# Two key loads split into bands of 112, 8 and 8 partitions in a two-layer decode kernel

## The chip, the cores and the metric

The kernel runs on one core of a Trainium2 chip. The metric is the device time of one execution in microseconds (us). The core has sixteen DMA engines that move data between the chip's main memory (HBM) and the on-chip memory of 128 partitions, and five instruction streams: TensorE (PE in the profile), VectorE (DVE), ScalarE (ACT), GpSimd (POOL) and SyncE (SP). In this kernel SP does nothing but issue DMA transfers.

## The reference

Two layers, each attention over a cached context followed by a gated MLP, are applied to two sequences of one new token each. The same weights serve both layers.

```python
def _A_ref(x, k_cache, v_cache, wq, wo):          # D = 576, H = 32, Sk = 8192, Dh = 128
    q = (x @ wq).reshape(B, Sq, H, Dh).transpose(0, 2, 1, 3)
    scores = einsum("bhqd,bhkd->bhqk", q, k_cache) * (Dh ** -0.5)
    p = softmax(scores)
    o = einsum("bhqk,bhkd->bhqd", p, v_cache)
    return o.transpose(0, 2, 1, 3).reshape(B, Sq, H * Dh) @ wo

def _B_ref(x, w_gate, w_up, w_down):              # Df = 4608
    return (gelu(x @ w_gate) * (x @ w_up)) @ w_down

x = x + _A_ref(layernorm(x), ...); x = x + _B_ref(layernorm(x), ...)
x = x + _A_ref(layernorm(x), ...); x = x + _B_ref(layernorm(x), ...)
```

The key cache and the value cache have 2 x 32 heads of 8192 x 128 float32 values, 256 MiB each, and both layers read all of them. With the weights that is over a gigabyte per execution, and each value is used once per layer, so the work per byte is small.

## The kernel before

The unit of attention work is an `Item`: one sequence and two neighbouring heads (30 items, `PAIRS`), or one head for the last four items. The keys of a pair are 8 MiB and land as a tile of 128 partitions, each of which holds 128 rows of 128 values, 64 KB in one piece. The values of a pair have the same form.

All large tiles live in one buffer, `space`, cut into slots by hand. The class `Arena` keeps account of which parts are free. The functions `plan_first`, `plan_second` and `plan_mlp` append loads to a list in the order in which they are to be issued; `pump` issues from its head for as long as the arena has room, and `done` frees a part and calls `pump` again. So the order of the loads on SP's queue is written out by hand, and each issue waits on SP until the work that last read its place in `space` has ended. In layer 0 the items go from 0 up, and the order is key n, then value n - 1. In layer 1 they go down: key n, then value n + 1. There is room for three pair tiles, so an 8-MiB load is issued while the one or two before it are still on their way.

For each item, VectorE multiplies the keys by the query (line 511), GpSimd adds the two halves of each row (line 515), and VectorE sums the rest (line 518). A short softmax follows on VectorE, TensorE and ScalarE, and TensorE multiplies the weights with the values (line 604). After the last item of a layer, the output weights (`out_rows`, line 281) are multiplied in at line 657, `add_to_x` adds to x, and the MLP streams gate, up and down weights (lines 228 to 263). In layer 0's MLP the gate and up weights are loaded by `split_rows` in transfers to every second partition (line 238).

The lines that the change touches are `load` (line 163, its DMA at line 166), which issues one transfer, `cache` (line 168), which makes the list entry for a whole item, and one call in each of `plan_first` and `plan_second`.

Of the kernel before, what the change touches and what calls it, by code (L numbers as in the profile page):

```python
# [15 lines left out]
P = 128  # L16
# [8 lines left out]
JC = 16  # L25
# [15 lines left out]
NPLACE = 4  # L41
RING = 5 * SLOT
END = RING + NPLACE * PLACE
HELD = 5


# [13 lines left out]
ITEMS = [Item(b, h, 2) for h in range(0, H - 2, 2) for b in range(B)]  # L60
# [7 lines left out]
class Arena:  # L68
# [38 lines left out]
    def fit(self, key, n, lo=0):  # L107

        for at in [self.at, lo] + sorted(end for _, end in self.live.values()):
            if lo <= at and at + n <= END and self.take(key, at, n) is not None:  # L110
                self.at = at + n
# [11 lines left out]
def decode_layers(ctx, tc, x_in, kc, vc, wq, wo, wg, wu, wd, out):  # L123
    nc = tc.nc
# [8 lines left out]

    space = consts.tile([P, END], F32, name="space")

    x = consts.tile([P, CW], F32, name="x")
    nc.vector.memset(x, 0.0)
    for c in range(4):
        for s in range(2):
            lo = 32 * c + s * B  # L140
# [16 lines left out]
    def part_at(at, n):  # L157
        return space[:, at:at + n]
# [1 line left out]
    def part(at):  # L160
        return part_at(at, PART).rearrange("p (j d) -> p j d", d=DH)

    def load(at, n, src, lo, hi):

        t = part_at(at, (hi - lo) * PART).rearrange("p (j d) -> p j d", d=DH)
        nc.sync.dma_start(t, ITEMS[n].source(src)[:, lo * JC:hi * JC, :])

    def cache(key, src, n, slots=None, pieces=None):

        parts = ITEMS[n].parts  # L170

        def make():
            at = arena.pair(key) if slots is None else arena.slots(key, slots, parts)
            if at is None:
                return False
            lo = 0
            for m in pieces or (parts,):
                load(at[lo], n, src, lo, lo + m)
                lo += m
            ready[key] = dict(enumerate(map(part, at)))  # L180
            places[key] = at
            return True

        queue.append(make)

    def half(key, src, n, k, slot):

        def make():
            at = arena.slots(key, (slot,), 4, k)
            if at is None:  # L190
                return False
            load(at[0], n, src, k, k + 4)
            ready.setdefault(key, {}).update((k + i, part(a)) for i, a in enumerate(at))
            return True

        queue.append(make)

    def one(key, src, n, k, where):

        def make():  # L200
            at = arena.ring((key, k), PART) if where is None else arena.take((key, k), places[where[0]][where[1]], PART)
            if at is None:
                return False
            load(at, n, src, k, k + 1)
            ready.setdefault(key, {})[k] = part(at)
            return True

        queue.append(make)
# [13 lines left out]
    def half_rows(key, w, us, first):  # L222

        width = w.shape[1] // 2
        rows = w.rearrange("r (s w) -> (r s) w", w=width).rearrange("(p u) w -> p u w", p=P)

        def transfers(t):
            nc.sync.dma_start(t.rearrange("p (u w) -> p u w", w=width), rows[:, us[0]:us[-1] + 1, :])

        weights(key, len(us) * width, first, transfers)  # L230
# [36 lines left out]
    def products():  # L267

        def make():
            at = [RING + k * PLACE for k in (2, 3)]  # L270
            if not all(arena.clear(a, PLACE) for a in at):
                return False
            ready["products"] = [part(arena.take(("products", k), at[k], PART)) for k in range(2)]
            return True

        queue.append(make)

    def out_rows(layer, g):

        rows = wo[g * GH * DH:(g + 1) * GH * DH, :].rearrange("(p i) c -> p (i c)", i=GH)  # L280
        weights(("wo", layer, g), GH * D, whole_at[layer], lambda t: nc.sync.dma_start(t, rows))
# [14 lines left out]
    def groups(layer):  # L296
        return range(H // GH)[::1 - 2 * layer]

    def name(kind, layer, n):

        return kind, 1 if n in (KEYS_HELD if kind == "k" else VALUES_HELD) else layer, n

    def plan_first():
        def k(n, *at):
            cache(name("k", 0, n), kc, n, *at)

        def v(n, *at):
            cache(name("v", 0, n), vc, n, *at)

        for us in WQ[0]:  # L310
            half_rows(("wq", 0, us[0]), wq, us, END - NU * H * DH // 2)
        last = PAIRS - 1
        k(0)
        for n in range(1, PAIRS):
            k(n)
            v(n - 1)
        k(SINGLE[0], (0,))
        half(("v", 0, last), vc, last, 0, 1)
        half(("v", 0, last), vc, last, 4, 5)
        k(SINGLE[1], (3,))  # L320
        v(SINGLE[0], (4,))

        k(SINGLE[2], (2,))
        products()
        k(SINGLE[3], (0,))
        v(SINGLE[1], (4,))
        v(SINGLE[2], (3,))
        for g in groups(0)[:2]:
            out_rows(0, g)
        v(SINGLE[3], (1,), (1,) * 4)  # L330
        for g in groups(0)[2:]:
            out_rows(0, g)

    def plan_second():
        for us in WQ[1]:
            half_rows(("wq", 1, us[0]), wq, us, None)
        last = PAIRS - 1
        k63, v63, k62, v62 = ("k", 1, SINGLE[3]), ("v", 1, SINGLE[3]), ("k", 1, SINGLE[2]), ("v", 1, SINGLE[2])
        for k in range(4):
            one(("k", 1, SINGLE[1]), kc, SINGLE[1], k, None)  # L340
        for k in range(4):
            one(("k", 1, SINGLE[0]), kc, SINGLE[0], k, (k63, k))

        for kind, k in (("k", 0), ("v", 0), ("v", 1), ("k", 1), ("v", 2), ("v", 3), ("k", 2), ("k", 3)):
            if kind == "k":
                one(("k", 1, last), kc, last, k, (k62, k))
            else:
                one(("v", 1, SINGLE[0]), vc, SINGLE[0], k, (v63, k))
        for k in range(4):
            one(("k", 1, last), kc, last, 4 + k, (v62, k))  # L350
        half(("k", 1, last - 1), kc, last - 1, 0, 5)
        half(("k", 1, last - 1), kc, last - 1, 4, 4)
        cache(("v", 1, last), vc, last)
        for n in range(last - 2, -1, -1):
            cache(("k", 1, n), kc, n)
            cache(("v", 1, n + 1), vc, n + 1)
        cache(("v", 1, 0), vc, 0, None, (4, 2, 1, 1))
        for g in groups(1):
            out_rows(1, g)

    def plan_mlp(layer):
# [11 lines left out]
        for rows in DOWN[layer]:  # L373
            down(layer, rows)

    plan_first()
    plan_mlp(0)
    plan_second()
    plan_mlp(1)
    pump()  # L380
# [453 lines left out]
```

## Time and profile before

| what | value |
|---|---|
| median of 3 runs | 2697.15 us (2696.98 to 2701.9) |
| the profiled execution | 2700.58 us, its span 2698.8 us |
| VectorE busy | 1872.1 us, 69% of the span |
| GpSimd busy | 1210.8 us, 45% |
| TensorE busy | 900.1 us, 33% |
| read from HBM | 1154.23 MB, 428 GB/s over the span |

The profile follows one execution. Its page gives each engine's busy time, the span in 40 slices with a digit for the busy share in tenths (9 is 90% or more), the DMA queues (q1 is the kernel's own hardware queue issued from SP; the two others that matter here, marked "instruction", fetch the engines' programs), and the chain of work that ended last, followed back from the end. In the chain and in the timelines a row begins with its start and its length in us. The DMA view can be asked for a window of the span; its digits and counts are then of that window, cut into 40 slices again. "Under 512 B" counts the smallest packets, nearly all of them the writes that report a transfer's completion.

### The profile page before, as it was taken

The numbers are of one execution on the slowest core, as the hardware profiler recorded it, in microseconds if no ns is written. First come the engines' busy times: TensorE is split into PE (matmuls) and PEld (weight loads), VectorE is DVE, ScalarE is ACT, GpSimd is POOL, SyncE is SP. The second block draws the span as 40 slices with busy tenths as digits, with TensorE's granted clock in tenths as the row PEclk, the third lists the DMA queues.
The fourth block names the chain that finished last, engine by engine and source line by source line (L and its number), as shares of the span: only waits on it lengthen the run. The fifth ranks groups of instructions, "written<-read, shape, count | busy, mean of one in ns | idle before, by whom it ended". The sixth has DMA issues, their size and how long they took to land.

```text
span 2698.8 us, 17988 instructions
## 1 busy us (share of the span) xinstructions
PE 900.1 (33%) x7020; PEld 294.0 (11%) x7020; DVE 1872.1 (69%) x1688; ACT 90.0 (3%) x399; POOL 1210.8 (45%) x528
## 2 busy tenths in 40 slices
PE   1323331333233223334644332333233323322355
PEld 0100010001000000111211110001000100000022
DVE  4877787678777776776039887778767867777740
ACT  0000000000000000000000000000000000000000
POOL 2644454445445444544016554445444544544420
PEclk7656656665666566666766665665566566656677
DMA  9999999999999999999999999999999999999998
GB/s 420 435 434 434 434 434 433 433 432 434 435 433 432 435 432 430 433 428 422 403 378 421 429 427 436 435 430 434 434 434 431 434 434 432 434 433 436 432 421 378
DMA packets 33524, 1155.39 MB, mean 428 GB/s; under 512 B 3976, under 2 KB 4000, under 8 KB 5536
## 3 DMA queue, kind: packets, MB, share of 16 engines
q1 hardware_dynamic: 33400, 1154.24, 99.5%
q8 instruction: 55, 0.90, 0.1%
q14 instruction: 29, 0.24, 0.0%
q10 hardware_dynamic: 40, 0.01, 0.0%
HBM read 1154.23 MB, written 0.00 MB: 428 GB/s over the span
## 4 chain that ended last, share of the span: by engine, by line
DMA 82%; DVE 15%; PE 1%; issue 1%; POOL 1%; ACT 0%; SPq 0%; ACTq 0%; DVEq 0%; POOLq 0%
DMA space<-in_A_k_cache_dram 75%; DVE space L511 9%; DVE S L518 5%; DMA space<-in_B_w_up_dram 3%; DMA space<-in_A_wo_dram 2%; DMA space<-in_B_w_down_dram 2%; POOL space L515 1%; DMA space<-in_A_wq_dram 1%; PE acc L742 0%; DMA space<-in_B_w_gate_dram 0%; DMA x<-in_A_x_dram 0%; PE xps L791 0%; PE acc L604 0%; PE acc L478 0%; DVE osb L620 0%
## 5 line engine op out<-in xcount | busy, mean ns | idle before, releaser
L515 POOL TENSOR_TENSOR space<-space 128x1024 f32<-128x1024 f32 x512 | 1206.8, 2357 | 1245.2 <-DVE space L511 1230.4
L511 DVE TENSOR_TENSOR space<-space,qp 128x2048 f32<-128x2048 f32 x512 | 1166.0, 2278 | 591.7 <-DMA space<-in_A_k_cache_dram 567.9
L604 PE MATMUL acc<-space,prz 128*8 128x512 f32 x4096 | 591.3, 740 | 452.2 <-DMA space<-in_A_v_cache_dram 447.6
L518 DVE TENSOR_REDUCE S<-space 128x16 f32<-128x1024 f32 x512 | 618.9, 1209 | 3.4 <-POOL space L515 3.4
L534 PE MATMUL mT<-ident,m 128*1 128x128 f32 x68 | 24.8, 365 | 804.9 <-DVE m L532 804.9
L604 PEld LDWEIGHTS acc<-space,prz 128*8 128x8 f32 x4096 | 118.2, 104 | 868.4 <-DMA space<-in_A_v_cache_dram 452.1
L563 ACT ACTIVATE nbs<-nb 64x1 f32<-64x1 f32 (+1 forms) x128 | 21.2, 166 | 2333.7 <-PE nb L542 2333.0
L534 PEld LDWEIGHTS mT<-ident,m 128*1 128x1 f32 x68 | 5.4, 79 | 821.9 <-issue 786.5
L629 PE MATMUL po<-of,osb 128*32 128x2 f32 x512 | 40.9, 202 | 130.9 <-DVE osb L620 130.9
L542 PE MATMUL nb<-m,unit 1*128 1x2 f32 (+1 forms) x136 | 39.2, 355 | 125.1 <-DVE m L540 125.1
L464 POOL TENSOR_TENSOR rstd<-ve,mhalf 128x1 f32<-128x1 f32 x4 | 2.2, 552 | 170.6 <-DVE ve L462 170.6
L620 DVE SCALAR_TENSOR_TENSOR osb<-acc,diag,osb 128x128 f32<-128x128 f32 x192 | 67.3, 351 | 6.8
L767 DVE STREAM_TRANSPOSE o<-o 128x288 f32<-128x288 f32 x4 | 2.8, 692 | 92.1 <-ACT o L765 92.1
L574 PE MATMUL tot<-sums,unit 128*128 128x2 f32 x120 | 35.2, 363 | 92.1 <-ACT prz L565 92.1
L499 PE MATMUL qp<-qsb,pick 4*64 4x128 f32 (+1 forms) x256 | 30.7, 304 | 80.6 <-DVE space L511 77.3
L468 DVE TENSOR_TENSOR x<-xps,x 128x144 f32<-128x144 f32 x4 | 1.2, 308 | 73.0 <-PE xps L791 42.2
L565 ACT ACTIVATE prz<-S,nbs 64x128 f32<-64x128 f32 (+1 forms) x128 | 50.7, 396 | 12.5 <-POOL prz L555 8.4
L629 PEld LDWEIGHTS po<-of,osb 128*32 128x32 f32 x512 | 35.7, 154 | 139.2 <-DVE osb L620 137.9
L542 PEld LDWEIGHTS nb<-m,unit 1*128 1x128 f32 x136 | 33.3, 303 | 146.3 <-DVE m L540 146.3
L574 PEld LDWEIGHTS tot<-sums,unit 128*128 128x128 f32 x120 | 30.1, 311 | 97.3 <-ACT prz L565 97.3
L791 PE MATMUL xps<-space,hT 128*4 128x144 f32 x576 | 29.8, 374 | 21.0 <-DMA space<-in_B_w_down_dram 19.4
L742 PE MATMUL acc<-space,xt 128*8 128x288 f32 x288 | 30.5, 564 | 18.9 <-DMA space<-in_B_w_up_dram 11.2
(62 smaller groups left out, 294.3 us busy)
## 6 DMA issues: line engine op xcount, KB each, us to landing
space<-in_A_k_cache_dram SPq DMA_DIRECT2D x6, 4096.0 KB
space<-in_A_v_cache_dram SPq DMA_DIRECT2D x6, 4096.0 KB
space<-in_A_wo_dram SPq DMA_DIRECT2D x16, 1152.0 KB
space<-in_A_k_cache_dram SPq DMA_DIRECT2D x16, 1024.0 KB
space<-in_B_w_down_dram SPq DMA_DIRECT2D x9, 1152.0 KB
space<-in_B_w_gate_dram SPq DMA_DIRECT2D x3, 3456.0 KB
space<-in_A_v_cache_dram SPq DMA_DIRECT2D x10, 1024.0 KB
space<-in_A_wq_dram SPq DMA_DIRECT2D x3, 3072.0 KB
```

Source lines behind the costliest of these rows:

```text
L499: nc.tensor.matmul(qb[n][to, :], pick[32 * c:32 * c + 4, r:r + 1].to_broadcast([4, P // it.heads]), qsb[32 * c:32 * c + 4, (h % 4) * DH:(h ...
L511: nc.vector.tensor_tensor(out=u, in0=t, in1=qb[n].unsqueeze(1).to_broadcast([P, JC, DH]), op=ALU.mult)
L515: nc.gpsimd.tensor_tensor(out=half, in0=half, in1=u[:, :, DH // 2:], op=ALU.add)
L518: nc.vector.tensor_reduce(out=S[n][:, k * JC:(k + 1) * JC], in_=prod.pop((n, k)), axis=AX.X, op=ALU.add)
L534: nc.tensor.transpose(mT[n], m, ident)
L542: nc.tensor.matmul(mT[n][:, :heads], ones[0:1, :], m1[:, :heads], start=True, stop=True)
L565: nc.scalar.activation(pr[at, lo:].rearrange("p (g e) -> p g e", e=4)[:, 0:it.rows // 2:2, :], s[at, :it.rows].rearrange("p (g r) -> p g r ...
L574: nc.tensor.matmul(tot[:, :it.heads], ones, rs.pop(n), start=True, stop=True)
L604: nc.tensor.matmul(accumulator(n)[32 * c:32 * c + 8, :], pr[:, at:at + 8], t[g // 4][:, g % 4 * 4:g % 4 * 4 + 4, :].rearrange("p j d -> p ...
L620: nc.vector.scalar_tensor_tensor(t, q[:, r, :], diag[:, r:r + 1], t, op0=ALU.mult, op1=ALU.add,)
L629: nc.tensor.matmul(po[lo:lo + 32, i, :], t[:, i::GH], of, start=True, stop=True)
L742: nc.tensor.matmul(acc[32 * c:32 * c + 4 * B, h, :HG], window(u, 4 * g + 2 * e), w[:, k, c, :], start=(key == steps[0][0] and k == 0), sto ...
```

## The change

`load` gets a parameter `bands`, a list of partition counts, and issues one transfer for each band instead of one for the whole tile. `cache` hands it on. The default is a single band of 128. Two loads, the key load of item 29 in layer 0 (the last pair there) and that of item 0 in layer 1 (the last item there), are given `UNEVEN`, the bands 112, 8 and 8. The three transfers go to the same places and read the same bytes as the one did; 112 partitions are seven packets of 64 KB for each of the sixteen DMA engines, and a band of eight is one packet for each of eight engines, so that in these two loads eight engines take nine packets and the other eight take seven.

```diff
+UNEVEN = (112, 8, 8)
...
-    def load(at, n, src, lo, hi):
+    def load(at, n, src, lo, hi, bands=(P,)):

         t = part_at(at, (hi - lo) * PART).rearrange("p (j d) -> p j d", d=DH)
-        nc.sync.dma_start(t, ITEMS[n].source(src)[:, lo * JC:hi * JC, :])
-
-    def cache(key, src, n, slots=None, pieces=None):
+        of_item = ITEMS[n].source(src)[:, lo * JC:hi * JC, :]
+        p = 0
+        for m in bands:
+            nc.sync.dma_start(t[p:p + m], of_item[p:p + m])
+            p += m
+
+    def cache(key, src, n, slots=None, pieces=None, bands=(P,)):
...
-                load(at[lo], n, src, lo, lo + m)
+                load(at[lo], n, src, lo, lo + m, bands)
...
         for n in range(1, PAIRS):
-            k(n)
+            cache(("k", 0, n), kc, n, bands=UNEVEN if n == last else (P,))
             v(n - 1)
...
         for n in range(last - 2, -1, -1):
-            cache(("k", 1, n), kc, n)
+            cache(("k", 1, n), kc, n, bands=UNEVEN if n == 0 else (P,))
             cache(("v", 1, n + 1), vc, n + 1)
```

## The prediction

> **What bounds the kernel now.** I read the page first (shares, slices, chain), then the chain in order of time around the two loads that change, then the sync queue's timeline, and last the DMA view in short windows.
>
> The page of before:
>
> ```profile
> span 2698.8 us, 17988 instructions
> ...
> DMA  9999999999999999999999999999999999999998
> ...
> q1 hardware_dynamic: 33400, 1154.24, 99.5%
> q8 instruction: 55, 0.90, 0.1%
> q14 instruction: 29, 0.24, 0.0%
> HBM read 1154.23 MB, written 0.00 MB: 428 GB/s over the span
> ...
> DMA 82%; DVE 15%; PE 1%; issue 1%; POOL 1%; ACT 0%; SPq 0%; ACTq 0%; DVEq 0%; POOLq 0%
> ```
>
> All sixteen DMA engines are busy in every slice, 99.5% of their time is spent on the kernel's own loads, and the work is fixed: 1154 MB. No compute engine matters: VectorE's 15% of the chain lies between a landing and the next issue, while the queues still hold work. What matters is how evenly the sixteen engines share the bytes, since a load has landed only when the slowest has written its part. Two small customers share the engines: 55 instruction fetches on q8 and 29 on q14.
>
> The chain of waits in order of time (start, length, what), around a steady stretch and the second changed load:
>
> ```profile
> 1978.78 36.22 DMA space<-in_A_k_cache_dram
> 2015.02 2.29 DVE space L511
> 2018.46 35.24 DMA space<-in_A_k_cache_dram
> ...
> 2484.88 35.24 DMA space<-in_A_k_cache_dram
> ...
> 2523.58 35.23 DMA space<-in_A_k_cache_dram
> 2558.83 2.29 DVE space L511
> ...
> 2593.80 21.58 DMA space<-in_A_wo_dram
> 2615.40 49.39 DMA space<-in_B_w_up_dram
> 2664.81 29.62 DMA space<-in_B_w_down_dram
> ```
>
> One round of an 8-MiB key and an 8-MiB value load takes 2523.58 - 2484.88 = 38.70 us, so one load 19.35 us. It has 128 partitions of 64 KB, eight to an engine, so one packet of 64 KB takes 19.35 / 8 = 2.42 us on its engine. That is the unit of all that follows. After the second changed load the chain is DMA to the end: whatever the slowest engine loses there, the end loses.
>
> Which engine is slowest can be read from the landings. The load issued at 1978.78 landed after 36.22 us, the next after 35.24. The DMA view of these two stretches:
>
> ```profile
> DMA packets 274, 15.80 MB, mean 434 GB/s; under 512 B 32, under 2 KB 32, under 8 KB 32
> ## 3 DMA queue, kind: packets, MB, share of 16 engines
> q1 hardware_dynamic: 273, 15.79, 100.4%
> q14 instruction: 1, 0.01, 0.1%
> ```
>
> ```profile
> DMA packets 264, 15.16 MB, mean 428 GB/s; under 512 B 32, under 2 KB 32, under 8 KB 32
> ## 3 DMA queue, kind: packets, MB, share of 16 engines
> q1 hardware_dynamic: 263, 15.14, 98.9%
> q8 instruction: 1, 0.02, 0.2%
> ```
>
> The stretch with a q14 fetch landed 0.98 us later; the one with a q8 fetch landed on time. So q14 fetches fall on the engine that is already last, q8 fetches on others that have room. The same step recurs in the second layer's chain:
>
> ```profile
> 2173.31 36.21 DMA space<-in_A_k_cache_dram
> ...
> 2367.80 36.20 DMA space<-in_A_k_cache_dram
> ```
>
> These three are 194.5 us apart: one sequencer fetching at its own pace through one DMA engine. The end of the run shows how far the engines have drifted apart (the DMA view of 2688.2 to 2696.2, slices of 0.2 us):
>
> ```profile
> DMA  9889756864776566554555674211000000000000
> ```
>
> At 2689 engines begin to stop, at 2691 to 2692.5 about half still work, at 2693 to 2693.8 one or two. The digits add up to 157 tenths, or 3.1 us of all sixteen: with perfect sharing they would stop at about 2691.5, so the whole gain to be had at this end is about 2.3 us.
>
> **The change, part by part.** In each layer one key load (pair 29 in layer 0, pair 0 in layer 1) becomes three: 112 partitions (seven packets for each engine) and twice 8 (one packet for each of eight engines). No byte, wait or compute instruction is added or removed; both engine orders differ only by the extra issues. In text: eight "takers" get nine packets, eight "givers" seven.
>
> *Issues.* Two more on the sync queue at each place. The sync queue's timeline:
>
> ```profile
> 1117.74 0.33 SPq L166 DMA_DIRECT2D space<-in_A_k_cache_dram  x1
> 1143.42 0.33 SPq L166 DMA_DIRECT2D space<-in_A_v_cache_dram  x1
> ...
> 2523.58 0.33 SPq L166 DMA_DIRECT2D space<-in_A_k_cache_dram  x1
> 2549.48 13.12 SPq L166 DMA_DIRECT2D space<-in_A_v_cache_dram  x5
> ```
>
> Each costs 0.33 us, 0.66 us per place. The next issue stands 25 us behind, and the load needs 19.35 of its 35.23 us, so 15.9 us of earlier work lies in the engines' queues while these go out. Cost 0; without that cover 2 x 0.66 = 1.3 us. The extra completion writes (a load makes 16 of the 32 small packets above; a band of eight should add eight) are two more on each taker: I take 0, with 0.1 us as the upper end.
>
> *Shares.* Each taker does one packet more per place, +2.42 us, each giver one less, -2.42 us. What this does to the time depends on which half holds the slowest engine, and no row names engines. Upper end: it is a taker, +2.42 per place. Lower end: it is a giver, at best -2.42. I take the taker. The q8 fetches fall on engines with room and the q14 engine is outside them, as the landings show; the change is sensible as a balance only if the seven-packet half holds the q8 engines, which leaves the q14 engine among the nine. That is a guess about numbering, worth about three to one. [...]
>
> *Does the first place count in full?* After layer 0 the chain still ends on loads:
>
> ```profile
> 1263.13 18.66 DMA space<-in_A_wo_dram
> 1283.30 9.61 DMA space<-in_A_wo_dram
> 1301.55 5.25 DMA space<-in_B_w_up_dram
> 1308.18 11.54 DMA space<-in_B_w_up_dram
> ```
>
> The output weights land 18.66 us after the last compute needed them: the slowest engine decides, so its 2.42 us go through to x and to the layer that follows. Late next is every later key load by the same 2.42 us. Lower end 0, if the drift is lost in the MLP; upper end 2.42. I take 2.42, since the links are continuous.
>
> Sum: 0 + 2.42 + 2.42 = 4.84 us. The profiled execution took 2700.58 us (span 2698.8, 1.8 around it) and would take 2705.4. It is 3.4 us above the median of the runs, 2697.15, so I forecast 2697.15 + 4.84 = 2702.0 us.
>
> **The rivals.**
>
> *1. The small bands queue at their destination (slower).* In a 128-partition load each engine has eight partitions of its own to write. In a band of eight, eight engines write eight neighbouring partitions at once. If neighbouring partitions are fed together, at no more than one packet per 2.42 us for a group, eight packets in g groups take 8/g x 2.42 us: 9.68 us with two groups, 19.35 with one, instead of 2.42. With two groups the takers lose 2 x 9.68 - 4.84 = 14.5 us beyond the 2.42, 16.9 per place, 33.8 in all: 2731 us; with one group 72.6 us: 2770. The 112-partition part, seven partitions to an engine and no longer eight, could collide too. With four groups it is 2 x (2 x 4.84 - 4.84) + 4.84 = 14.5 us, or 2711.7, and from there down it decides; I price the rival at the middle, two groups. For it: the sixteen engines run at one common rate, which could be either side's. Against: the split weight loads write every second partition, another pattern, at full rate (DMA view of 1313 to 1322):
>
> ```profile
> DMA packets 515, 3.83 MB, mean 425 GB/s; under 512 B 100, under 2 KB 100, under 8 KB 100
> ```
>
> but they load all partitions' neighbourhoods alike, so that clears little. [...]
>
> *2. The slowest engine is a giver.* Then it ends 2.42 us earlier, but takers move 2.42 us the other way: those that stop around 2691 now stop near 2693.4, against 2693.8. Between 0 and 2.42 us gained per place, half of it on average: 2697.15 - 2.4 = 2694.7 us. It needs the q14 engine and the q8 engines on the same half. 0.2% is out of reach: that is 5.4 us, and both places together cannot give more than 4.84.
>
> *3. The change does not do what it says.* If engines are chosen by destination partition, each keeps its eight packets whatever the bands, and only the issues are new, under cover: 2697.2 us.
>
> **How the numbers follow.** Forecast (slowest is a taker, no queueing): 0.42, own range 2700.5 to 2703.5. Rival 1: 0.36, from 2711 to 2770. Rival 2: 0.12. Rival 3: 0.06. Anything unforeseen that is faster: 0.04. The range 2694 to 2740 holds the forecast, rivals 2 and 3 and the part of rival 1 up to somewhat over two groups. A change under 0.2% (5.4 us) cannot be told from none with this kernel's three runs between 2696.98 and 2701.9. Slower by over 0.2%: rival 1 and about four tenths of the forecast, whose 4.84 lies just inside the bound, 0.36 + 0.18 = 0.54. Same: the rest of the forecast, rivals 2 and 3, 0.42. Faster: 0.04.
>
> **What would show it.** The list of issues should show two key loads of 7168 KB and four of 512 KB. Right: in the chain the key loads issued near 1117.7 and 2523.6 land 2.4 us later than their neighbours (37.65 in place of 35.23), later rounds keep 38.70, and the last slices end in a longer tail with one or two engines. Rival 1: those landings are late by 10 us and more and the GB/s slices behind them sink well under 430. Rival 2: landings earlier by up to 2.4 us. Rival 3: nothing moves. I am wrong if the two places cost differently, or if a stretch of idle DMA in the first MLP swallows the first 2.42 us.

## The result, and the profile after

The changed kernel takes 2769.74 us (median of 5 runs, 2766.75 to 2771.61), against 2697.64 us before: a ratio of 1.0258, 95% interval 1.0246 to 1.027, or 72 us slower. The forecast was 4.84 us slower, 2702.0, with a range up to 2740.

The page of after (span, the DMA lines by slice, the queues, the chain's shares):

```profile
span 2769.0 us, 18000 instructions
...
DMA  9999999999999999999999999999999999999998
GB/s 424 436 428 435 435 432 433 433 430 434 435 434 428 436 432 431 271 393 416 391 366 425 436 428 435 435 433 431 433 434 436 429 435 428 436 436 428 242 423 353
...
q1 hardware_dynamic: 33432, 1154.24, 99.2%
...
HBM read 1154.23 MB, written 0.00 MB: 417 GB/s over the span
...
DMA 78%; DVE 15%; another core or an unknown queue 3%; PE 2%; issue 1%; POOL 1%; SPq 0%; ACT 0%; ACTq 0%; DVEq 0%; POOLq 0%
```

The rate by slice in the page of before:

```profile
GB/s 420 435 434 434 434 434 433 433 432 434 435 433 432 435 432 430 433 428 422 403 378 421 429 427 436 435 430 434 434 434 431 434 434 432 434 433 436 432 421 378
```

The same bytes, the same full DMA row of nines, and yet two slices in which the rate sinks: 271 GB/s in the seventeenth and 242 in the thirty-eighth, where before had 433 and 432. They hold the two changed loads. The digits alone would hide it. A DMA engine counts as busy for as long as its packet takes, so the rate has to be read beside the share (0.98 busy at 218 GB/s, in the table by stage below). The new entry in the chain, "another core or an unknown queue", is no other core: nearly all of it (44.60 and 43.68 us, below) is VectorE waiting for a load that is now three transfers, which the profile puts down to no single one of them.

The sync queue's timeline and the chain in order of time give the length of that wait:

```profile
1117.58 1.09 SPq L170 DMA_DIRECT2D space<-in_A_k_cache_dram  x3
...
2559.48 1.04 SPq L170 DMA_DIRECT2D space<-in_A_k_cache_dram  x3
```

```profile
1078.87 35.24 DMA space<-in_A_k_cache_dram
1114.11 0.02 issue
...
1143.27 44.60 another core or an unknown queue
```

```profile
2520.77 35.24 DMA space<-in_A_k_cache_dram
...
2585.17 43.68 another core or an unknown queue
```

Before, the same load took half as long:

```profile
1117.74 35.23 DMA space<-in_A_k_cache_dram
```

The load issued at 1117.58 is there at 1143.27 + 44.60 = 1187.87, after 70.3 us; its neighbour took 35.24. The second takes 2628.85 - 2559.48 = 69.4 us. That is 35.1 and 34.1 us more, together 69 of the 72.

The table by stage around the first place (the last two columns are DMA share and GB/s):

```profile
1114.00:1124.00 10.00, 1.54 (x5) 1.08 (x5) 9.80 (x10) 1.31 (x6) 4.99 (x3) 0.50 0.97 419
1124.00:1132.00 8.00, 0.64 (x8) 0.56 (x8) 7.89 (x9) 0.00 (x0) 4.41 (x2) 0.50 1.13 312
1132.00:1160.00 28.00, 9.10 (x66) 1.98 (x66) 11.27 (x8) 0.00 (x0) 9.43 (x4) 0.68 0.98 218
1160.00:1177.00 17.00, 0.00 (x0) 0.00 (x0) 0.00 (x0) 0.00 (x0) 0.00 (x0) 0.50 1.15 173
1177.00:1184.00 7.00, 0.00 (x0) 0.00 (x0) 0.00 (x0) 0.00 (x0) 0.00 (x0) 0.50 0.64 159
1184.00:1207.00 23.00, 2.18 (x13) 1.63 (x13) 18.84 (x19) 1.31 (x6) 10.23 (x5) 0.50 0.97 415
```

Nothing is idle in DMA from 1132 to 1160, and yet 218 GB/s is half of the usual 434. Against 434 the four middle rows lose 8 x (1 - 312/434) = 2.2, 13.9, 10.2 and 4.4 us, 30.8 of the 35.1. The first of the two large ones is mostly the time of the 112 partitions, in which every engine has seven packets; the second is mostly that of the bands of eight.

The trace also keeps the start and the length of every packet, and they show what the shares cannot. The records name no engine, but each packet begins within 0.1 us of the end of another, which links them into sixteen chains, one for each engine. Outside the two places nearly every packet of 64 KB takes 2.42 us.

At the first place the seven packets of the 112 took 32.7 to 36.6 us on each engine, 4.83 us apiece on average, and the sixteen packets of the two bands took 4.8 to 7.9 us each. The loads beside the pieces were held up too: on the eight engines that carry no band, the eight packets of the value load behind took 27.4 to 35.0 us instead of 19.4. On the engine that finished last, the eight packets of the load ahead took 24.7 us, the seven of the 112 took 36.6, and its two of the bands 7.0 and 5.0. That is 73.2 us where sixteen packets of 2.42 us took 38.7 before, 34.5 us more, nearly all of the 35.1. That engine never stopped, and neither did the others: the low share of 0.64 from 1177 to 1184 is no empty queue, since a window counts a packet with its whole length where it starts, and packets were up to 8 us long here.

### The profile page after: what moved, and what is told of

The parts are those of the page before. It is cut to its first block, busy times and chain, and to the rows that moved or that the text cites. A ratio compares the mean times of both kernels' runs of the same rounds, so it can differ in the third digit from the quotient of the medians.

```text
span 2769.0 us, 18000 instructions
## 1 busy us (share of the span) xinstructions
PE 908.2 (33%) x7020; PEld 296.9 (11%) x7020; DVE 1872.2 (68%) x1688; ACT 90.0 (3%) x399; POOL 1210.0 (44%) x528
## 4 chain that ended last, share of the span: by engine, by line
DMA 78%; DVE 15%; another core or an unknown queue 3%; PE 2%; issue 1%; POOL 1%; SPq 0%; ACT 0%; ACTq 0%; DVEq 0%; POOLq 0%
DMA space<-in_A_k_cache_dram 70%; DVE space L516 9%; DVE S L523 5%; DMA space<-in_B_w_down_dram 2%; DMA space<-in_A_wo_dram 2%; DMA space<-in_B_w_gate_dram 2%; DMA space<-in_B_w_up_dram 1%; DMA space<-in_A_wq_dram 1%; POOL space L520 1%; PE xps L796 0%; PE acc L609 0%; PE acc L747 0%; DMA x<-in_A_x_dram 0%; DVE osb L625 0%
## 5 line engine op out<-in xcount | busy, mean ns | idle before, releaser
L747 PE MATMUL acc<-space,xt 128*8 128x288 f32 x288 | 32.8, 603 | 16.9 <-DMA space<-in_B_w_up_dram 10.7
```

Of the source, the lines that this page charges most:

```text
L747: nc.tensor.matmul(acc[32 * c:32 * c + 4 * B, h, :HG], window(u, 4 * g + 2 * e), w[:, k, c, :], start=(key == steps[0][0] and k == 0), sto ...
```

## The experiments

Two theories stood at the start. *Destination*, the assumption of the prediction's rival 1: partitions are fed in groups, each at one packet per 2.42 us, and a transfer that does not spread over all groups is slow. *Shares*: only the number of packets per engine counts. A third, *source*, puts the slowness of the new pieces on the pattern of addresses that is read. All ratios are to the kernel before, run on the same chip beside the experiment.

### Where it is slow: four ways to halve a load

Edits to the two changed loads, relative to the changed kernel. The first needs no more than the constant; in the other three the destination and the source are halves or alternate partitions in turn.

```diff
-UNEVEN = (112, 8, 8)
+UNEVEN = (64, 64)
...
+        lower, alternate = [slice(0, HALF), slice(HALF, P)], [slice(e, P, 2) for e in range(2)]
+        for to, at in zip(alternate, alternate):       # e2; (lower, alternate) e3; (alternate, lower) e4
+            nc.sync.dma_start(t[to], of_item[at])
```

> The two key loads go out as partitions 0 to 63 and then 64 to 127, four packets for each engine and transfer, so the shares are even. Theory 'destination' (partitions lie in groups that take one packet per 2.42 us, and a stretch of 64 neighbours reaches half of the groups): each of the eight packets takes 4.84 us, 19.4 us more per place, 38.7 in all: about 2736 us. Theory 'source' (the pattern of addresses read from HBM is what slowed the 112): the same time as the kernel that reads halves and writes alternate partitions. Theory 'shares' (only the number of packets per engine counts): 2697.6 us.

> The two key loads go out as the even and then the odd partitions, read from the same alternate rows. Destination: every transfer reaches all groups, no loss, 2697.6 us. Source: the same time as the kernel that reads alternate rows and writes halves. Shares: 2697.6 us.

> The transfers write partitions 0 to 63 and 64 to 127 but read the even and the odd rows (the keys of these two items land in other partitions than they should, so their scores are of other rows; the work is the same). Destination: about 2736 us, as with halves on both sides. Source: as with alternate rows on both sides. Shares: 2697.6 us.

> The transfers write the even and the odd partitions but read the lower and the upper 64 rows (keys of these two items land in other partitions, the work is the same). Destination: 2697.6 us, as with alternate partitions on both sides. Source: as with halves on both sides. Shares: 2697.6 us.

| written | read | time, us | ratio (95%) |
|---|---|---|---|
| halves | halves | 2758.21 | 1.021 (1.0195 to 1.0225) |
| alternate | alternate | 2701.16 | 0.9999 (0.999 to 1.0009) |
| halves | alternate | 2757.99 | 1.0209 (1.0194 to 1.0224) |
| alternate | halves | 2701.66 | 1.0002 (0.9993 to 1.0011) |

(Before, on that chip: 2701.44.) The time follows what is written and not at all what is read. That settles destination against source. It also removes shares as the cause of the 72 us: with halves every engine has its even eight packets, and 57 us are lost all the same. The stage of 1132 to 1160, halves first and then alternate (here 1132 to 1150), from the tables of these two kernels:

```profile
1132.00:1160.00 28.00, 9.32 (x66) 2.04 (x66) 11.50 (x8) 0.00 (x0) 9.42 (x4) 0.68 1.01 206
```

```profile
1132.00:1150.00 18.00, 10.34 (x66) 2.16 (x66) 11.60 (x8) 0.00 (x0) 9.46 (x4) 0.69 1.06 459
```

206 GB/s at a DMA share of 1.01, against 459 (a short window counts packets where they start, so it can lie a little over 434). The loss was 28 us per place where packets alone gave 19.4. Half of a 434 GB/s rate would be 217, so 206 explains only a part of the rest. The packet records show the remainder in the load ahead: on the engine that finished last, the eight packets of the halves took 39.7 us, and the eight ahead of them 27.1, each in place of 19.4. Together that is 28.1 us.

### Shares by themselves

All loads whole, and behind the two key loads a copy from HBM to HBM, which has no partition as its destination:

```diff
+            if extra:
+                nc.sync.dma_start(spare[:EXTRA, :JC * DH * 8], ITEMS[n].source(src)[:EXTRA].rearrange("p j d -> p (j d)"))
```

> All loads as before, 128 partitions each; behind the same two key loads a copy of 8 rows of 64 KB from HBM to a spare place in HBM is added (its result is used by nothing), one packet for each of eight engines and no partition as its destination. It shows the shares by themselves. If the slowest engine is one of the eight, as the forecast had it: the key load's successor lands 2.4 us later at each place, 2.4 + 2.4 = 4.8 us, about 2702.4 us against 2697.6. If it is one of the other eight: the eight move 2.4 us nearer to it and the time moves by less than 1 us per place. In both cases nothing near the 72 us of the changed kernel.

> The same with 16 rows, one more packet for each of the sixteen engines: whichever engine is slowest, 2.4 us per place, 4.8 in all, about 2702.4 us. The yardstick for the copy of eight rows.

Eight rows: 2706.44 us, ratio 1.0022 (1.0012 to 1.0031). Sixteen rows: 2706.15, ratio 1.002 (1.001 to 1.0029); before, on that chip, 2700.02. So one packet more on eight engines costs as much as one more on all sixteen, about 6 us for two places where 4.84 was expected, which lies within the interval. The slowest engine is among the eight that take the extra packet. The packet records of the changed kernel agree: at both places, the engine that finishes last is one that carries two band packets. This is the forecast's own sum, and it held; it was 5 of 72 us.

### Which partitions are written together

> The two key loads go out as eight transfers of 16 neighbouring partitions, one packet for each engine and transfer. [...] Theory 'transfers' (each further transfer costs the same): twice what quarters cost. Shares: 2700 us.

> Four transfers of 32 neighbouring partitions. [...] Neighbourhood (the more neighbours a transfer covers, the faster): twice the loss of the halves, 2810 us. Transfers: three further transfers where the halves had one, 2870 us.

> Eight transfers of 16 partitions, every eighth one. No two are neighbours. [...] Neighbourhood: no loss, 2700 us. Transfers: as the blocks of 16.

> Four transfers of 32 partitions, every fourth one. [...] Transfers: as the quarters.

The edits: the constant at `(16,) * 8` and `(32,) * 4`; for the last two the loop writes `t[e::8]` and `t[e::4]` from the same rows.

| transfers of each load | time, us | ratio (95%) |
|---|---|---|
| two of 64 neighbours (above) | 2758.21 | 1.021 (1.0195 to 1.0225) |
| four of 32 neighbours | 2758.73 | 1.0221 (1.0205 to 1.0236) |
| eight of 16 neighbours | 2787.89 | 1.0333 (1.0313 to 1.0353) |
| eight of every eighth | 2753.24 | 1.0201 (1.0186 to 1.0216) |
| four of every fourth | 2700.99 | 1.0005 (0.9995 to 1.0014) |

(Before, on the chip of the last four: 2699.42.) Quarters cost what halves cost, 59 us against 57. Every eighth partition, without a neighbour in the transfer, loses about as much, 54 us, and every fourth loses nothing. So neither being neighbours nor the number of transfers is what costs; the time follows which partitions a transfer writes. How many groups there are, and which partitions would belong to one, these five runs do not show.

The blocks of 16 lost 88 us, the most of all these splits, though less than the author's estimate, which rested on a number of groups that no run shows. Their tables:

```profile
1132.00:1160.00 28.00, 9.49 (x66) 2.05 (x66) 11.53 (x8) 0.00 (x0) 9.40 (x4) 0.68 1.02 143
1160.00:1177.00 17.00, 0.00 (x0) 0.00 (x0) 0.00 (x0) 0.00 (x0) 0.00 (x0) 0.50 1.07 154
1177.00:1190.00 13.00, 0.00 (x0) 0.00 (x0) 0.00 (x0) 0.00 (x0) 0.00 (x0) 0.50 1.00 136
```

They moved 136 to 154 GB/s, about a third of 434. The packet records show that an engine goes on to its next block without waiting for the others: at 1158 us the sixteen engines stood in four different blocks, the second to the fifth, and a packet took 7.3 us on average, three times 2.42.

### Even shares, and one place alone

> The two key loads go out as 112 and 16 partitions: seven and one packets for each of the sixteen engines, so the shares are even, eight each. [...] Shares: 2697.6 us, as nothing is uneven.

> The changed kernel with the bands of 112, 8 and 8 in layer 1 alone. If the two places cost the same and neither is swallowed later: half of 72 us, about 2733.6 us. If the first place is partly lost in the first MLP: more than half, up to 2769.

112 and 16 partitions (`UNEVEN = (112, 16)`): 2757.66 us, ratio 1.0213 (1.0199 to 1.0228). Eight packets for every engine, and still 58 us lost: evenness does not prevent the loss. The bands in layer 1 alone: 2733.74 us, ratio 1.0124 (1.0109 to 1.0138), 33.7 us where half of the whole is 36. The two places cost about the same, and the first MLP swallows nothing.

### The parts by themselves

Each of these kernels leaves out a part of the two key loads, whose partitions keep what an earlier load left there. The last one brings two bands of eight partitions that lie fourteen apart (0, 14 to 98, and 1, 15 to 99).

```diff
-        p = 0
-        for m in bands:
-            nc.sync.dma_start(t[p:p + m], of_item[p:p + m])
-            p += m
...
+            nc.sync.dma_start(t[0:112], of_item[0:112])                         # e13
+            for p in (112, 120): nc.sync.dma_start(t[p:p + 8], of_item[p:p + 8])   # e14
+            for p in (0, 1): nc.sync.dma_start(t[p:p + 112:14], of_item[p:p + 112:14])   # e15
```

> The two changed loads bring partitions 0 to 111 alone; the last 16 keep what an earlier load left there, so those scores are of other rows. Theory 'the 112 is the larger part': its seven packets take 4.84 us each, 33.9 us in place of the 19.4 of the whole load, 14.5 us more per place; with the neighbouring loads disturbed as by the halves (9 us per place) up to 23.5: 2728 to 2746 us. Theory 'the bands of eight are the loss, the 112 is harmless': seven packets of 2.42, 2.4 us less per place, 2695 us.

> The two changed loads bring only the two bands of eight (112 to 119 and 120 to 127); the other 112 partitions keep what an earlier load left. Eight engines have two packets where they had eight, the others none. Two groups per band, as the prediction priced it: 2 x 9.7 = 19.4 us, what the whole load took, so no gain: 2699 us, more if they disturb their neighbours. No queueing: 4.8 us in place of 19.4, 14.5 less per place, 2670 us, if the shorter load shows at all.

> [...] If eight engines on eight partitions are slow by themselves: the same as the neighbouring bands.

The 112 alone: 2738.35 us, ratio 1.0145 (1.013 to 1.016); before, on that chip, 2699.72. So 38.6 us, 19.3 per place, are lost though an eighth of the load is not even fetched. Its table:

```profile
1132.00:1160.00 28.00, 9.91 (x66) 2.10 (x66) 11.41 (x8) 0.00 (x0) 9.43 (x4) 0.62 0.99 222
1160.00:1177.00 17.00, 0.37 (x1) 0.08 (x1) 4.87 (x4) 0.00 (x0) 2.35 (x1) 0.50 0.95 308
```

222 GB/s from 1132 to 1160, half rate, as in the changed kernel; the seven packets took 32.4 to 33.6 us on each engine. From 1160 to 1177, where the changed kernel has its bands and moves 173 GB/s, this one is back to 308. Of the changed kernel's 36 us per place the 112 makes 19.3, and the two bands add 36 - 19.3 = 16.7.

The bands alone gave 2702.05 us, ratio 1.0007 (0.9998 to 1.0017), and the spread bands 2697.13, ratio 0.9988 (0.9979 to 0.9998), far from the 2670 that the bands without queueing were expected to give. Both times are inconclusive in size, also where the first meets what two groups per band would give: with 7 MiB gone the engines ran out of work, because the next value load still waits on the sync queue for its place. The spread bands' tables show the hole:

```profile
1124.00:1132.00 8.00, 0.64 (x8) 0.56 (x8) 7.87 (x9) 0.00 (x0) 4.50 (x2) 0.50 0.94 321
1132.00:1140.00 8.00, 1.87 (x12) 0.44 (x16) 8.00 (x7) 0.00 (x0) 5.67 (x3) 0.50 0.16 57
1140.00:1150.00 10.00, 7.50 (x65) 1.89 (x53) 9.97 (x9) 0.15 (x1) 6.81 (x4) 0.96 0.30 105
```

For 18 us the DMA share is 0.16 to 0.30. What tells the two apart is, first, the chain: with neighbouring bands VectorE waits for the load until 1118.06 + 27.21 = 1145.27, with spread bands it does not wait for it at all.

```profile
1118.06 27.21 DMA space<-in_A_k_cache_dram
```

Second, the packets: at this first place the sixteen of the neighbouring bands took 4.72 us on average (2.48 to 6.83), those of the spread bands 3.21 (2.42 to 4.74), and several of these only the usual 2.42. So bands of neighbours are the slower ones here too, but by less than the 9.68 us that two groups per band would give.

No version that brings the whole load beats the kernel before. The best splits are equal to it, as a single transfer of 128 partitions already runs at 434 GB/s, and a packet more on eight engines cost as much as one on all sixteen.

## Why the prediction was wrong

*What bounds the kernel* held. The chain and the unit of 2.42 us per packet were read rightly; the rate by slice shows that lost DMA time is lost time. One reading was too wide: not every q14 fetch falls on the slowest engine. The window from 2407.4 to 2442.8 of the run before holds one as well, and its key load landed after 35.23 us, on time.

*Issues* held: three issues in 1.09 and 1.04 us, with the next one 30.7 us behind at the first place, and no engine ran dry.

*Shares*, with the guess that the slowest engine is a taker, held: about 6 us by the extra copies, 4.84 forecast. *The first place counts in full* held too: 33.7 us for the second alone out of 72.

*The step that failed* is the choice of the likeliest case, that a packet takes 2.42 us wherever it goes. In the pieces it took 4.83 us on average in the 112 and 4.8 to 7.9 in the bands, and it slowed the packets of the loads beside it. The 2.42 us were measured in loads of all 128 partitions, the only ones in the long stretches of the trace, and I carried the price over to pieces of a tile. The evidence that I held against queueing, the split weight loads at 425 GB/s, is a load of alternate partitions: the experiments show that this form loses nothing (ratio 0.9999), and so it could not speak for 112 neighbours. I said that it clears little, and still gave no queueing the larger chance.

*Rival 1* named the right side, the destination, and was sized by half. Its price for the two bands, two packets of 9.68 us, is 19.4 us on top of the 112, where the runs leave 16.7. Two groups to a band is a term that no run shows. That the two sums lie so close is partly luck: the band packets took 4.8 to 7.9 us, and the rest is time that they cost other packets, which the rival left out. The other half was named in one sentence, "the 112-partition part ... could collide too", and given no price: 19.3 us per place, and 218 GB/s in the table by stage. Seven packets at twice 2.42 us are 7 x 2.42 = 16.9 us more, though the factor of two comes from the runs and stood in no row before them. That with the rival's 16.9 for the bands would have been 2 x (16.9 + 16.9) = 67.8 us, or 2765. A term that is only "could" belongs in the sum of its rival, at a bound; left out, it put the range's upper end 30 us too low. (That the rival's one-group price came to 2770 is chance: the band packets took 4.8 to 7.9 us, not 19.35.)

*Rivals 2 and 3* are refuted: the slowest engine is a taker, and the packet records of the changed kernel show nine packets of the load on eight engines and seven on the other eight.

*What would show it*: landings later by 10 us and more and GB/s well under 430 was the sign given for rival 1, and both are there. The list of issues, though, does not show the new sizes; it puts all large key loads in one line, now four more:

```profile
space<-in_A_k_cache_dram SPq DMA_DIRECT2D x62
```

## What to carry to other kernels

A transfer of part of the partitions has its own price. In these runs two loads of 8 MiB split into pieces of 64 or 32 neighbours cost 57 and 59 us, into every eighth partition 54, into blocks of 16 88, and into every second or fourth partition nothing (ratios 0.9999 and 1.0005). The size of a piece does not tell its price: the 112 ran at 218 GB/s and 64 neighbours at 206, both about half of 434, where every fourth partition, 32 to a piece, moved 459 (1132 to 1150, a short window). So before splitting a load, time the pieces in question and read their GB/s. Allow for the loads beside the pieces as well, whose packets slow down too (with the halves, 27.1 us for the eight ahead in place of 19.4). If a load must be split by partitions, try every second or fourth partition first, the two forms that lost nothing here, and not blocks. And a balance of packets over DMA engines worth 2 us per load is not to be bought with pieces that run at half rate, as the 112 did.

## What the runs showed that was not expected

Engines stayed fully "busy" at half the rate, 0.98 to 1.01 of their time at 206 to 222 GB/s, because each packet took twice as long: 4.83 us on average in the 112, in place of 2.42. Seven-eighths of the partitions ran little better than a half of them: 112 neighbours went at 218 GB/s, 64 at 206. Which partition each engine writes at each moment in that transfer does not show in the profile, and no run varied the spacing or the source of the 112 itself, so why it is just half stays open.
